# Ten dummy matmuls ahead of the transpose of c and seven behind it, with the ones tile written by VectorE

## Chip, cores and metric

One core of a Trainium2 chip. The metric is the device time of one execution in microseconds (us). Every execution of the experiments is also recorded with its span (first to last instruction, about 1.7 us less than the time) and its mean granted TensorE clock; one execution of each kernel has a full trace.

## The reference

An attention block with sliding-window KV cache and an MLP, both with layer norm modulated by a small vector c. Only the head of it matters here: no projection of x can start before both the normalized x and the modulation from c are there.

```python
mod = (_silu(c) @ w_mod).reshape(c.shape[0], 6, 1, -1)
sa, ca, ga, sb, cb, gb = (mod[:, 0], ..., mod[:, 5])        # cut
h = _layernorm(x, axis=-1) * (1 + ca) + sa
x = x + ga * _A_ref(h, A_k_cache, A_v_cache, A_wq, A_wo)     # 2048 x 512, 32 heads, window 512
h = _layernorm(x, axis=-1) * (1 + cb) + sb
x = x + gb * _B_ref(h, B_w1, B_w2)
```

## The kernel before

Each engine runs its own list, in program order (in the trace before GpSimd has silu at 5.43, 5.80 and 6.92 us, then the pow at 7.08); waits come from the tiles that an operation reads and writes (PE waits 0.73 us for `c_row`). In the views PE is TensorE, PEld its weight loads, DVE VectorE, ACT ScalarE, POOL GpSimd and SP SyncE, which issues loads. This is the opening, up to the first projection (cuts marked). `warm(n)` is n dummy matmuls that keep TensorE busy while the first loads are under way; their result is never read.

```python
def warm(n):
    for i in range(n):
        mm(bank[WBK], ones[:, :], ones[:, 0:1].to_broadcast([P, QB]), True, True, [R_ones], [WBK], i == n - 1)

def silu_exp(bk):                      # c as a row -> c as a column, exp(-c) and c
    cT = bank[bk].bitcast(BF)[:, 0:DC]
    kb.op(PE, ... e.transpose(cT, c_row[:, :], ident[0:DC, 0:DC]) ...)
    kb.op(ACT, ... e.activation(tmp[:, :], cT, ACTF.Exp, scale=-1.0) ...)
    kb.op(ACT, ... e.activation(c_f[:, :], cT, ACTF.Copy) ...)

def silu_mul():                        # three operations on GpSimd
    kb.op(POOL, ... tmp = min(tmp, 1e38) + 1 ...)
    kb.op(POOL, ... tmp = tmp ** -1 ...)
    kb.op(POOL, ... sc_bf = c_f * tmp ...)

# ... loads: x (tiles 0, 1) on SP, x (tiles 2, 3) on ACT, c on SP, then w_mod, wq, k, v
kb.op(POOL, lambda e: e.memset(ones[:, :], 1.0), writes=[R_ones])
# ... identity and other constants on POOL
warm(7)
silu_exp(5)
warm(9)
# ... statistics of x tile 3 on ACT
silu_mul()
ln_stat(0); ln_stat(1); rstd_add(0, 2); rstd_pow(0, 2)   # DVE, DVE, DVE, POOL
ln_stat(2); rstd_add(2, 3); rstd_pow(2, 4)
ln_norm(0); ln_norm(1)                 # DVE: xn of tiles 0 and 1
# ... xn of tile 3 on POOL
ln_tposes(0, TB[0])                    # PE: four transposes of xn, "psS<-ident,xn"
for f in mod_cols_mm(0, QBK): f()      # PE: 32 one-column matmuls, "psQ<-sc_bf,wmw"
# ... modulation, then the first projection, "psQ<-hT,wq", and the first scores
```

GpSimd takes `silu_mul` first and `rstd_pow(0, 2)` after it (at 7.08 us, though the pow's input was there at 6.70), and `ln_norm(0)` waits for that pow. So the first normalized tile waits for c, although it doesn't use it.

Of the kernel before, what the change touches and what calls it, by code (L numbers as in the profile page):

```python
# [1198 lines left out]
def build_fast(nc, es, top, A_x, A_k_cache, A_v_cache, A_wq, A_wo, B_x, B_w1, B_w2, c, w_mod, out, flag):  # L1199
# [28 lines left out]
    def T(name, shape, dt=BF):  # L1228
        return es.enter_context(nc.sbuf_tensor(name, shape, dt))
# [26 lines left out]
    ones = T("ones", [P, P])  # L1256
# [30 lines left out]
    kb = KB(nc)  # L1287
    PE = kb.stream("pe", sem("s_pe"))
    ACT = kb.stream("act", sem("s_act"))
    DVE = kb.stream("dve", sem("s_dve"))  # L1290
    POOL = kb.stream("pool", sem("s_pool"))
# [22 lines left out]
    R_ident, R_ones, R_c, R_sc, R_scf, R_tmp, R_cst = (Res(n) for n in ("ident", "ones", "c", "sc", "scf", "tmp", "cst"))  # L1314
# [27 lines left out]
    def load_v(g, eng=None):  # L1342
        dma(v_sb[:, g, :, 0:Dh], A_v_cache[0][g, Sk - W:, :].rearrange("(k p) d -> p k d", p=P), f"v{g}", writes=[R_v[g]], eng=eng)
# [27 lines left out]
    def mm(out_ap, lhsT, rhs, start, stop, reads, bk, signal):  # L1371
        kb.op(PE, lambda e: e.matmul(out_ap, lhsT, rhs, start=start, stop=stop), reads=reads, group_writes=[R_b[k] for k in bk], signal=signal)  # L1372
# [4 lines left out]
# [3 lines that stand above are left out]
# [34 lines left out]
    def silu_exp(bk):  # L1414
        cT = bank[bk].bitcast(BF)[:, 0:DC]
        kb.op(PE, lambda e: e.transpose(cT, c_row[:, :], ident[0:DC, 0:DC]), reads=[R_c, R_ident], group_writes=[R_b[bk]])  # L1416
        kb.op(ACT, lambda e: e.activation(tmp[:, :], cT, ACTF.Exp, scale=-1.0), reads=[R_b[bk]], writes=[R_tmp])
        kb.op(ACT, lambda e: e.activation(c_f[:, :], cT, ACTF.Copy), reads=[R_b[bk]], writes=[R_cf])
# [146 lines left out]
    load_wq(2, 2)  # L1565
    load_k(0)
    load_v(0)
    kb.op(POOL, lambda e: e.memset(ones[:, :], 1.0), writes=[R_ones])
    kb.op(POOL, lambda e: e.memset(cst[:, 0:1], -0.5), writes=[R_cst])
    kb.op(POOL, lambda e: e.affine_select(ident[:, :], ones[:, :], pattern=[[1, P]], compare_op=ALU.is_equal, fill=0.0,  # L1570
                                          base=0, channel_multiplier=-1), reads=[R_ones], writes=[R_ident])
# [3 lines left out]
    kb.op(POOL, lambda e: e.memset(m01[:, 0:DC], 0.0), writes=[R_m01])  # L1575
    kb.op(POOL, lambda e: e.memset(m01[:, DC:2 * DC], 1.0), writes=[R_m01])
    kb.op(ACT, lambda e: e.activation(cst[:, 2:3], cst[:, 0:1], ACTF.Exp), reads=[R_cst], writes=[Res("dummy")])
    warm(7)
    silu_exp(5)
    warm(9)  # L1580
    t3 = TPB - 1
    kb.op(ACT, lambda e: e.activation(xn[:, t3, :], x_sb[:, t3, :], ACTF.Copy, accum_out=s3[:, 0:1]), reads=[R_x[t3]], writes=[R_xn[t3], R_s3])
    kb.op(ACT, lambda e: e.activation(s3[:, 1:2], s3[:, 0:1], ACTF.Copy, scale=-1.0 / D), reads=[R_s3], writes=[R_s3])
# [217 lines left out]
def bass_adaLN_cond__sliding_block_cached__dense_activation_relu__prompt_kernel(  # L1801
# [14 lines left out]
    with ExitStack() as top:  # L1816
        flag = top.enter_context(nc.sbuf_tensor("flag", [1, 8], mybir.dt.int32))
        with ExitStack() as es:
            kb, fast, cut, dma_cnt, flag_ev = build_fast(nc, es, top, *args, flag)
            sems = dict(kb.sems)  # L1820
            meet = top.enter_context(nc.semaphore("s_meet"))
# [71 lines left out]
```

## Time and profile before

| | before |
|---|---|
| time, the 3 runs known when predicting | 561.12, 560.35, 560.62 us |
| the execution that has the trace | 561.10 us, span 559.4 |
| PE busy | 550.5 us, 98% of the span |
| first dummy / transpose of c / first transpose of xn / first projection | 1.04 / 4.95 / 8.82 / 10.86 us |

In the lines, the first number is the start in us, the second the length; brackets hold idle time of the engine before it and what ended it.

### The profile page before, as it was taken

To read this page: it belongs to the slowest core of one execution; us is meant where nothing else is said; L and a number is where in the kernel's file an instruction comes from. 1 tells how busy PE (TensorE), PEld (TensorE's weight loads), DVE (VectorE), ACT (ScalarE), POOL (GpSimd) and SP (SyncE) were. 2 spreads that over 40 slices of the span, in tenths; PEclk is the share of its full clock that TensorE was granted. 3 is DMA by queue.
4 is the path that set the end of the run, shared out by engine and by line. 5 is a ranking of instruction groups with operands and counts; after the bars stand their busy time and mean duration, and the time that the engine had idled before them with its cause. 6 is when DMAs were issued, how large, how long until landed. Compare 5 with 4: busy or idle time off the path is not lost.

```text
span 559.4 us, 9666 instructions
## 1 busy us (share of the span) xinstructions
PE 550.5 (98%) x4060; PEld 315.8 (56%) x4134; DVE 253.8 (45%) x551; ACT 348.9 (62%) x453; POOL 54.7 (10%) x53
## 2 busy tenths in 40 slices
PE   8999999999999999999999999999999999999998
PEld 4665555555555555555555555555555654444444
DVE  4455555553546544335445443333354448321134
ACT  4986666666666666666666666666666644432500
POOL 3000022004410000033000000332000000000000
DMA  9897763513114144352352412111215110210001
GB/s 268 248 207 174 143 169 46 114 39 76 40 38 76 39 73 117 58 133 57 94 95 57 76 40 39 39 39 38 39 39 76 39 30 0 44 34 23 22 29 47
DMA packets 113309, 42.67 MB, mean 76 GB/s; under 512 B 93928, under 2 KB 112104, under 8 KB 113256
## 3 DMA queue, kind: packets, MB, share of 16 engines
q1 hardware_dynamic: 112024, 40.82, 34.3%
q10 hardware_dynamic: 1232, 1.15, 0.6%
q8 instruction: 33, 0.54, 0.4%
q14 instruction: 20, 0.16, 0.1%
HBM read 18.35 MB, written 2.10 MB: 37 GB/s over the span
## 4 chain that ended last, share of the span: by engine, by line
PE 98%; issue 1%; DMA 1%; DVE 0%; SPq 0%; DVEq 0%
PE psS L1372 28%; PE psO L1372 27%; PE psQ L1372 23%; PE psW L1372 20%; DMA c_row<-in_c_dram 1%; DVE qT L1611 0%; DVE hT L1630 0%; SPq L1303 0%; DVE PT L1723 0%; DVE PT L1725 0%; PE psS L1375 0%; PE psO L1416 0%; DVE modc L1438 0%; DVEq L123 0%
## 5 line engine op out<-in xcount | busy, mean ns | idle before, releaser
L1493 ACT ACTIVATE PT<-psS 128x1024 bf16<-128x1024 f32 x256 | 262.7, 1028 | 128.2 <-PE psS L1372 128.1
L1372 PE MATMUL psS<-qT,kT 128*128 128x512 bf16 x508 | 150.9, 379 | 0.5 <-DVE qT L1611 0.4
L1372 PEld LDWEIGHTS psO<-v,PT 128*128 128x128 bf16 x2048 | 126.6, 98 | 30.2
L1372 PE MATMUL psO<-v,PT 128*128 128x129 bf16 x2048 | 137.0, 220 | 0.0
L1372 PE MATMUL psQ<-hT,wq 128*128 128x512 bf16 (+1 forms) x510 | 130.5, 377 | 0.3 <-DVE hT L1630 0.2
L1503 DVE RECIPROCAL rinv<-psO 128x4 f32<-128x4 f32 x128 | 23.3, 182 | 227.2 <-PE psO L1372 227.2
L1372 PE MATMUL psW<-wo,oT 128*128 128x512 bf16 x454 | 118.1, 379 | 3.0
L1504 DVE TENSOR_TENSOR o<-psO,rinv 128x512 bf16<-128x512 f32 x128 | 88.5, 691 | 4.9 <-DVE rinv L1503 0.5
L1372 PEld LDWEIGHTS psQ<-hT,wq 128*128 128x128 bf16 x512 | 49.9, 98 | 60.3 <-issue 0.6
L1372 PEld LDWEIGHTS psS<-qT,kT 128*128 128x128 bf16 x512 | 49.5, 98 | 58.9 <-ACT PT L1493 0.7
L1485 ACT ACTIVATE qT<-psQ 128x512 bf16<-128x512 f32 x126 | 74.7, 593 | 0.0
L1712 ACT ACTIVATE wq<-psS 128x512 bf16<-128x512 f32 x56 | 33.4, 597 | 49.3 <-PE psS L1372 48.9
L1372 PEld LDWEIGHTS psW<-wo,oT 128*128 128x128 bf16 x512 | 45.0, 98 | 32.9 <-DVE acc L1526 1.2
L1526 DVE TENSOR_TENSOR acc<-psW,acc 128x512 f32<-128x512 f32 x48 | 33.2, 691 | 6.5 <-PE psW L1372 6.5
L1372 PE MATMUL psO<-wmw,wq 128*128 128x512 bf16 (+1 forms) x165 | 32.8, 352 | 0.3
L1529 POOL TENSOR_TENSOR acc<-acc,gaf 128x512 f32<-128x512 f32 x12 | 15.6, 1303 | 146.7 <-DVE acc L1526 139.8
L1388 POOL TENSOR_TENSOR rstd<-rstd,cst 128x4 f32<-128x4 f32 x7 | 7.2, 1025 | 216.8 <-DVE rstd L1387 216.8
L1723 DVE TENSOR_TENSOR PT<-psO,gbf 128x512 f32<-128x512 f32 (+1 forms) x12 | 7.5, 624 | 40.4 <-PE psO L1372 40.4
L1372 PE MATMUL psS<-h2T,wmw 128*128 128x512 bf16 x109 | 25.0, 379 | 0.2
L1372 PEld LDWEIGHTS psO<-wmw,wq 128*128 128x128 bf16 x168 | 15.3, 98 | 16.5
L1372 PE MATMUL psS<-hT,wmw 128*128 128x512 bf16 x110 | 24.4, 379 | 0.1
L1382 DVE BATCH_NORM_STATS2 st<-x 128x6 f32<-128x512 bf16 x31 | 21.1, 681 | 4.8 <-DMA x<-in_A_x_dram 4.8
(85 smaller groups left out, 192.6 us busy)
## 6 DMA issues: line engine op xcount, KB each, us to landing
wo<-in_A_wo_dram SPq DMA_DIRECT2D x4, 1024.0 KB, 5.9
wq<-in_A_wq_dram SPq DMA_DIRECT2D x7, 512.0 KB, 4.6
wmw<-in_B_w_dram SPq DMA_DIRECT2D x14, 256.0 KB, 3.1
wmw<-in_w_mod_dram SPq DMA_DIRECT2D x5, 512.0 KB, 4.8
oT<-o SPq DMA_TRANSPOSE x128, 2.4
out_dram<-PT SPq DMA_DIRECT2D x15, 128.0 KB, 1.7
x<-in_A_x_dram SPq DMA_DIRECT2D x3, 512.0 KB, 4.3
v<-in_A_v_cache_dram SPq DMA_DIRECT2D x8, 128.0 KB, 3.8
```

The lines of the kernel that those rows point to most:

```text
L1372: kb.op(PE, lambda e: e.matmul(out_ap, lhsT, rhs, start=start, stop=stop), reads=reads, group_writes=[R_b[k] for k in bk], signal=signal)
L1382: kb.op(DVE, lambda e: e.bn_stats(st[:, t, :], x_sb[:, t, :]), reads=[R_x[t]], writes=[R_st[t]])
L1388: kb.op(POOL, lambda e: e.tensor_tensor(rstd[:, sl], rstd[:, sl], cst[:, 0:1].to_broadcast([P, hi - lo]), op=ALU.pow), reads=R_rstd[sl] + ...
L1485: kb.op(ACT, lambda e: e.activation(qT[u % NQT][:, :], bank[bk], ACTF.Copy), reads=[R_b[bk]], writes=[R_qT[u % NQT]])
L1493: kb.op(ACT, lambda e: e.activation(PT[u % NPT][:, pr * 2:pr * 2 + 2, :], s_ps[pr][:, :, :], ACTF.Exp, scale=scale), reads=[R_b[pr * 2], R ...
L1503: kb.op(DVE, lambda e: e.reciprocal(rinv[:, u, :], o_ps[:, :, P]), reads=[R_b[5], R_b[6]], writes=[R_rinv])
L1504: kb.op(DVE, lambda e: e.tensor_tensor(o_sb[u % NOS][:, :, :], o_ps[:, :, 0:P], rinv[:, u, :].unsqueeze(2).to_broadcast([P, TPB, P]), op=A ...
L1526: kb.op(DVE, lambda e: e.tensor_tensor(acc[:, tl, :], bank[WBK], acc[:, tl, :], op=ALU.add), reads=[R_b[WBK], R_acc[tl]], writes=[R_acc[tl]])
L1529: kb.op(eng, lambda e: e.tensor_tensor(acc[:, tl, :], acc[:, tl, :], gaf[:, :], op=ALU.mult), reads=[R_acc[tl], R_ga], writes=[R_acc[tl]])
L1712: kb.op(ACT, lambda e: e.activation(h1T[b % 2][:, fc, :], bank[bk], ACTF.Relu), reads=[R_b[bk]], writes=[R_h1[b % 2][fc]], pre=all_events( ...
L1723: kb.op(DVE, lambda e: e.tensor_tensor(yt[i][:, c0:c1], bank[bk][:, c0:c1], gbf[:, c0:c1], op=ALU.mult), reads=[R_b[bk], R_gb], writes=[R_ ...
```

## The change

Its intent, as I read it: no gap in TensorE's dummies while c is on its way, so that the clock opens sooner; that a gap keeps it shut was an estimate, which e1 and e10 test. "Open" is what the traces show as a change of pace: dummies start 0.43 us apart at first ("cold"; 7.59, 8.02, 8.45 in the weight loads of the trace before) and 0.22 us apart later ("hot").

```diff
-    kb.op(POOL, lambda e: e.memset(ones[:, :], 1.0), writes=[R_ones])
+    kb.op(DVE, lambda e: e.memset(ones[:, :], 1.0), writes=[R_ones])
@@
+    warm(10)
+    silu_exp(5)
     warm(7)
-    silu_exp(5)
-    warm(9)
```

## The prediction

> **What bounds the kernel now.** I read the page first: PE is busy for 550.5 of 559.4 us and 98% of the chain that ended last is PE, so the body of the kernel is a stream of matmuls that this change does not touch. Only the opening can move: dummy matmuls and the transpose of c are all issued in the first 9 us. So the second view is the chain of work that ended last, in order of time, for the opening:
>
> ```profile
> 1.24 3.66 DMA c_row<-in_c_dram
> 4.90 0.05 issue
> 4.95 0.18 PE psO L1416
> 5.13 3.86 PE psW L1372 x9
> 8.98 0.22 PE psS L1375 x4
> 9.21 0.79 PE psQ L1372 x32
> 10.00 0.02 issue
> 10.02 0.18 DVE modc L1438
> ...
> 10.30 0.42 DVE hT L1630
> ...
> 10.86 0.78 PE psQ L1372 x4
> ```
>
> Columns: start, length, what. c lands at 4.90 us, PE transposes it, then runs nine dummies (psW), and only then the four transposes of the first normalized tile (psS), the 32 one-column matmuls of the modulation (psQ), their eviction (modc) and the first real projection. So the nine dummies, meant only to warm PE, are on the path for 3.86 us. Was their follower ready earlier? The timeline tells:
>
> ```profile
> 1.04 3.17 PE L1372 MATMUL psW<-ones 128*128 128x512 bf16 x7 [1.04 <-POOL cst L1569]
> 4.95 0.18 PE L1416 MATMUL psO<-ident,c_row 4*128 4x4 bf16 x1 [0.73 <-DMA c_row<-in_c_dram]
> 5.06 3.92 PE L1372 MATMUL psW<-ones 128*128 128x512 bf16 x9
> 5.16 0.17 ACT L1417 ACTIVATE tmp<-psO 128x4 f32<-128x4 bf16 x1 [1.43 <-PE psO L1416]
> 5.43 0.28 POOL L1421 TENSOR_SCALAR tmp<-tmp 128x4 f32<-128x4 f32 x1 [3.17 <-ACT c_f L1418]
> 6.92 0.20 POOL L1423 TENSOR_TENSOR sc_bf<-c_f,tmp 128x4 bf16<-128x4 f32 x1
> 7.08 1.51 POOL L1591 TENSOR_TENSOR rstd<-rstd,cst 128x2 f32<-128x2 f32 x2
> 7.59 0.15 PEld L1372 LDWEIGHTS psW<-ones 128*128 128x128 bf16 x1 [0.28 <-issue]
> 7.82 1.22 DVE L1393 TENSOR_SCALAR xn<-x,mv,rstd 128x512 bf16<-128x512 bf16 x3
> 8.02 0.15 PEld L1372 LDWEIGHTS psW<-ones 128*128 128x128 bf16 x1 [0.28 <-issue]
> 8.45 0.15 PEld L1375 LDWEIGHTS psS<-ident,xn 128*128 128x128 bf16 x1 [0.28 <-DVE xn L1393]
> 8.82 0.39 PE L1375 MATMUL psS<-ident,xn 128*128 128x128 bf16 x4
> 9.04 0.94 PE L1372 MATMUL psQ<-sc_bf,wmw 128*128 128x1 bf16 x32
> ```
>
> The first of three DVE xn takes 0.41 us, so the tile is ready at 7.82 + 0.41 = 8.23, but its transposes start at 8.82: PE is late by 0.59 us, because it is still in dummies. The dummies are slow: weight loads are 0.43 us apart (7.59, 8.02, 8.45). Afterwards PE is about twice as fast: 4 transposes start within 9.04 - 8.82 = 0.22 us, 55 ns each.
>
> [...] By pace the clock opened during the last dummy, near 8.8 us. (The granted clock of the profile says 1.00 everywhere, so it cannot show this.) [...] The trace has no DVE memset to compare; on POOL it is 0.20.
>
> **The change part by part.**
> 1. The ones tile: POOL's 0.20 us at 0.78 goes to DVE, which has nothing to do until x lands at 4.79. Some 0.2 us there too, as small DVE rows take 0.16 to 0.18. The first dummy stays at about 1.04, give or take 0.1. POOL and the identity come no later than now, 3 us before they are needed.
> 2. Ten dummies before c: ten cold ones at 0.427 from 1.04 end at 5.31. c lands at 4.90, so its transpose moves from 4.95 to about 5.31, by +0.36. Gap gone.
> 3. Behind it the c chain moves by that 0.36: exp on ACT, then POOL's silu (5.43 to 7.12), and, since POOL works in order, its pow for rstd at 7.08 (its input, from DVE, was ready at 6.53 + 0.17 = 6.70). So the first xn is ready at 8.23 + 0.36 = 8.59 and its transposes may start at about 8.65.
> 4. Seven dummies behind c: [...] 7 x 0.216 = 1.5 us end near 6.9. Even if all seven stayed cold, 5.4 + 7 x 0.427 = 8.4, still ahead of 8.65. So PE now waits for xn, not xn for PE.
> 5. Sum on the path: transposes at 8.65 in place of 8.82, -0.17 us. Then 0.22 + 0.81 us to modc, as now; DVE's third xn ends at 9.04 + 0.36 = 9.40, before modc at 9.85. POOL's fourth xn (8.70 + 0.90) ends at 9.96, and is used by the last four transposes only, whose consumers sit behind DVE's other hT work. The rest of the opening slides with it: the loads have landed (wq issued at 1.72 took 7.3 us, kT at 2.62 at most 7.2, so 9.0 and 9.8, against uses at 10.8 and 13.1).
> 6. [...] The three times spread over only 0.77 us, so such losses must be rare or small; I allow a further 0.25 us for the median.
>
> Total: 560.62 - 0.17 - 0.25 = 560.2 us.
>
> **Rivals.** (a) The c chain wins: only its delay counts. For it: POOL's silu and pow are serial and begin 0.36 later. Against it: 0.59 us of slack at the transposes. If c lands late or the first dummy starts late, the gain turns into a loss of 0.1 to 0.3: 560.8. (b) PE goes cold again: warm dummies end near 6.9 and PE idles 1.7 us until 8.65[...]: 562. I give this 12%. (c) The whole 0.59 us or more comes out[...]: the transpose of c would then stay near 4.95 and xn near 8.25: 560.0. (d) Nothing is seen, because times of one kernel differ by 0.77 us: likely as to the verdict, and 560.6.
>
> **Range and chances.** The path gains 0.2 to 0.6 us, 0.1% of the time, next to a spread of 0.77. I say 560.2, from 559.4 to 561.0. The whole opening before the first attention scores is 13.3 us, 2.4% of the time; 2% is 11.2 us and cannot be won or lost there by shifting dummies. Hence 0.99 for within 2%, and a half per cent on each side.
>
> **What would show it.** Right: in the timeline of the changed kernel no idle before the transpose of c, which starts at 5.2 to 5.4; dummies behind it 0.22 us apart, from the first or after a few; an idle PE before the first psS transpose, ended by DVE xn, with that transpose at 8.5 to 8.7; POOL's silu beginning 0.3 to 0.4 later than 5.43; the first attention scores (psS from qT, 13.34 now) 0.2 us earlier. Wrong: dummies still 0.43 apart to the end, transposes or half projections at twice their pace (rival b), or first scores at or after 13.34. A move by more than 2 us would have to come from outside the opening, and I would have missed it altogether.

The sum came to 560.62 - 0.17 - 0.25 = 560.2 us. The -0.17 stands on the trace. The -0.25 (executions whose clock opens later, with part of the transposes and projections cold before the change and none after it): read it, like the 562 us of rival (b), as my estimate alone. Rival (c) meant an execution whose ten dummies end before 5.31. The two paces, which differ about twofold for 512 columns, come from the trace before: 0.427 us is a seventh of the time between the weight loads at 5.46 and 8.45, 0.216 a quarter of the 0.86 us of the four 512-column matmuls at 14.59 (`--critical`).

## The result, and the profile after

The changed kernel takes 561.33 us (median of 6 runs, 560.79 to 562.01), the kernel before 560.46 (6 runs, 560.09 to 561.12). The ratio is 1.0014, 95% interval 1.0001 to 1.0027: within 2%, but slower, and outside my range. One of the six has a granted clock of 0.997 (562.01). Ratios here are the mean time of one kernel's fast runs over that of the other's in the same rounds, so not quite the ratio of these medians.

The traced executions say the opposite: 560.80 us after, 561.10 before. The chain of work that ended last, changed kernel:

```profile
1.10 4.24 PE psW L1372 x10
5.34 0.12 PE psO L1416
...
5.48 0.17 ACT tmp L1417
5.66 0.07 ACT c_f L1418
...
5.75 0.28 POOL tmp L1421
...
6.12 1.05 POOL tmp L1422
...
7.24 0.20 POOL sc_bf L1423
7.44 0.67 POOL rstd L1591
...
8.13 0.43 DVE xn L1393
...
8.61 0.40 PE psS L1375 x4
...
10.66 0.78 PE psQ L1372 x4
```

and two rows of its timeline:

```profile
5.38 1.70 PE L1372 MATMUL psW<-ones 128*128 128x512 bf16 x7
8.61 0.40 PE L1375 MATMUL psS<-ident,xn 128*128 128x128 bf16 x4 [1.53 <-DVE xn L1393]
```

Nearly all that I forecast for this trace is there: ten dummies up to the transpose of c, which starts at 5.27 (I said 5.31); the seven behind it at open clock, 1.70 us; PE then idle 1.53 us until xn; its transposes at 8.61 (8.65); the first projection 0.20 us earlier than in the trace before (0.17). And yet the kernel is slower. So I suspected that the trace before is not what the kernel before usually does.

### The profile page after: what moved, and what is told of

Read it like the earlier page. It is cut to its first block, busy times and chain, and to the rows that moved or that the text cites. A ratio compares the mean times of both kernels' runs of the same rounds, so it can differ in the third digit from the quotient of the medians.

```text
span 559.1 us, 9668 instructions
## 1 busy us (share of the span) xinstructions
PE 549.3 (98%) x4061; PEld 315.5 (56%) x4135; DVE 254.1 (45%) x552; ACT 348.9 (62%) x453; POOL 54.6 (10%) x52
## 4 chain that ended last, share of the span: by engine, by line
PE 98%; issue 1%; DVE 0%; POOL 0%; ACT 0%; DVEq 0%; POOLq 0%
PE psS L1372 28%; PE psO L1372 27%; PE psQ L1372 23%; PE psW L1372 20%; POOL tmp L1422 0%; POOL rstd L1591 0%; DVE qT L1611 0%; DVE xn L1393 0%; DVE hT L1630 0%; PE psS L1375 0%; DVE PT L1723 0%; DVE PT L1725 0%; POOL tmp L1421 0%; POOL sc_bf L1423 0%; DVE modc L1438 0%
```

## The experiments

Theories. PIN: usually c is transposed before 4.95 and the dummies behind it run fast, so the chain from c bounds the opening; ten dummies pin the transpose at 5.3. DROP: PE's new idle stretch from 7 to 8.6 us makes the clock fall back in some executions. BODY: the difference lies after the opening. Thirteen experiments ran, three of them repeats of the two kernels, with 5 or 6 timed runs each, all results correct. "Before" stands for runs of the kernel before in the same rounds.

One table of all the traces first, as every experiment is read from it. Times in us; "x" and "c" are the landings of the load of x tiles 0 and 1 and of c, from the trace's record of finished transfers; "cT" is the start of the transpose of c, "xn" of the first ln_norm, "tp" of its first transpose on PE, "proj" of the first projection.

| run | dummies | this execution | x | c | cT | xn | tp | proj |
|---|---|---|---|---|---|---|---|---|
| before | 7/9 | 561.10 | 4.76 | 4.90 | 4.95 | 7.82 | 8.82 | 10.86 |
| after | 10/7 | 560.80 | 5.11 | 4.46 | 5.27 | 8.13 | 8.61 | 10.66 |
| e1 | 7/9 | 560.61 | 4.68 | 4.72 | 4.77 | 7.64 | 8.11 | 10.16 |
| e2 | 10/7 | 561.02 | 4.68 | 4.61 | 5.37 | 8.23 | 8.70 | 10.75 |
| e3 | 10/14 | 561.82 | 4.62 | 4.68 | 5.49 | 8.36 | 9.23 | 11.27 |
| e4 | 7/9 | 560.28 | 4.68 | 4.66 | 4.71 | 7.57 | 8.04 | 10.09 |
| e5 | 7/7 | 560.37 | 4.85 | 4.53 | 4.58 | 7.70 | 8.16 | 10.21 |
| e6 | 10/9 | 560.68 | 4.80 | 4.64 | 5.15 | 8.02 | 8.49 | 10.54 |
| e7 | 13/7 | 562.09 | 4.69 | 4.50 | 6.55 | 9.42 | 9.89 | 11.94 |
| e9 | 8/9 | 560.33 | 4.61 | 4.50 | 4.57 | 7.45 | 7.92 | 9.97 |
| e10 | 4/9 | 561.53 | 4.78 | 4.67 | 4.71 | 7.63 | 8.64 | 10.94 |
| e11 | 7/9, split | 560.47 | 4.77 | 4.48 | 4.53 | 7.62 | 8.08 | 10.13 |
| e12 | 10/7 | 562.09 | 4.76 | 4.93 | 4.97 | 7.84 | 8.31 | 10.36 |
| e13 | 8/7 | 560.43 | 4.76 | 4.63 | 4.68 | 7.61 | 8.07 | 10.12 |

(e8 changes the loads and stands apart below.) In all fourteen rows xn starts 2.84 to 2.87 us after the later of x and cT. Two chains of equal length meet there: x through VectorE's statistics, c through GpSimd. Then tp follows xn by 0.46 to 0.48 us, except in three rows (before, e3, e10), where PE was still in dummies.

### e1 and e2: both kernels again, unchanged

> The kernel before once more, unchanged, for a second trace and the granted clock of every run. Theory PIN (the transpose of c was only as late as in the first trace because c landed late there; in other runs c lands earlier, and the ten dummies of the change pin the transpose at 5.3 us): c lands before 4.9 us here, its transpose starts right after it, first attention scores before 13.34 us, span below 559.4 us, clock 1.000. Theory DROP (in the changed kernel PE idles from 6.9 to 8.6 us and in some runs the clock is taken back): nothing to see in this kernel, clock 1.000 in all runs, median 560.3 to 560.6 us. Theory BODY (the difference lies after the opening): span minus start of first scores differs from 546.0 us.

> The changed kernel once more. PIN: transpose of c at 5.3 us again whatever the landing of c, first scores at 13.1 us again, all runs near 560.8, clock 1.000, so the runs would spread little. DROP: runs split by granted clock; those at 1.000 take 560.8 us, those at 0.997 to 0.999 take 0.5 to 1.3 us more; median about 561.3. BODY: span minus start of first scores above 546.0 us.

e1 took 560.44 us (560.01 to 560.61), e2 560.99 (560.71 to 561.12), all ten runs at clock 1.000; the runs of before alongside 560.50, one of its eleven at 562.07 with clock 0.997. TensorE in the timeline of e1, the same kernel as the trace before:

```profile
1.04 3.17 PE L1372 MATMUL psW<-ones 128*128 128x512 bf16 x7 [1.04 <-POOL cst L1569]
4.77 0.18 PE L1416 MATMUL psO<-ident,c_row 4*128 4x4 bf16 x1 [0.56 <-DMA c_row<-in_c_dram]
4.88 2.13 PE L1372 MATMUL psW<-ones 128*128 128x512 bf16 x9
8.11 0.40 PE L1375 MATMUL psS<-ident,xn 128*128 128x128 bf16 x4 [1.09 <-DVE xn L1393]
```

The nine dummies take 2.13 us, not 3.92: the clock was open when they began, in spite of a gap of 0.56 us. PE is free at 7.0 and waits 1.09 us for xn. So the dummies that I saw on the path aren't there in this execution; the path is c, silu, pow, xn, and it gives the first projection at 10.16, 0.59 before e2's 10.75. That is PIN, to the size: cT is 0.60 later in e2. BODY falls: from the first projection to the end of the last matmul it is 546.05 us in e1 and 545.86 in e2.

### e4: VectorE's memset alone

```diff
-    kb.op(POOL, lambda e: e.memset(ones[:, :], 1.0), writes=[R_ones])
+    kb.op(DVE, lambda e: e.memset(ones[:, :], 1.0), writes=[R_ones])
```

> Only the memset of ones moved to VectorE; 7 and 9 dummies as before. First dummy at 1.10 in place of 1.04 us, seven end 0.06 later, still before c lands, so all theories: same as the kernel before within 0.1 us. If it is slower by 0.5 us or more, the memset is the cause and both PIN and DROP fall.

560.36 us (560.22 to 560.69), ratio to before 0.9997 (0.9984 to 1.0010). The first dummy starts at 1.10 in place of 1.04, the transpose of c at its landing. The interval alone would leave room for 0.56 us; the trace doesn't (first projection at 10.09), and e13 below keeps the memset without the loss. So the memset has no part in it.

### e6 and e7: ten ahead, thirteen ahead

```diff
-    warm(7)          # e6: ones on GpSimd, 9 behind
+    warm(10)
```
```diff
-    warm(10)         # e7: from the changed kernel
+    warm(13)
```

> The kernel before with 10 dummies ahead of the transpose of c in place of 7; 9 behind, memset of ones on GpSimd as before. PIN: c transposed at 5.3 to 5.4, xn and first projection 0.5 to 0.6 later than in the kernel before (10.7 against 10.1), median 561.0, clock 1.000. DROP: PE idles less than in the changed kernel (two dummies more), so nearer to before, 560.5.

> The changed kernel with 13 dummies ahead of the transpose of c in place of 10. PIN: three more dummies at 0.22 (clock open by then) to 0.43 us (not yet open) push the transpose of c to 6.0 to 6.7 us, and every later step of the chain by the same 0.65 to 1.3: median 561.6 to 562.2. DROP: PE idles as long as in the changed kernel; no more slow runs than there, and no other loss, since the last dummy ends before xn is ready: 561.0 to 561.3.

e6: 560.92 us (560.32 to 561.06), before 560.53. e7: 562.35 (562.09 to 562.71), ratio 1.0034 (1.0021 to 1.0047). In e7's chain of work that ended last, everything hangs on the thirteen dummies:

```profile
1.11 5.51 PE psW L1372 x13
...
9.42 0.42 DVE xn L1393
```

The dose fits PIN: cT goes 4.77, 5.15, 6.55 in e1, e6, e7, the first projection 10.16, 10.54, 11.94, so 5.39 after cT each time. e7's median lies a little over the range I gave it: two of its five runs have a dropped clock (0.997; 562.63 and 562.71), and the median of the other three is 562.20, the edge of the range. In its trace the dummies ran cold to the twelfth: cT is 1.28 us later than in the trace after, 0.43 for each of the three dummies more. DROP expected e6 near 560.5 and e7 near 561; both are off.

### e5 and e3: the number behind c

```diff
-    warm(9)          # e5: 7 ahead, ones on GpSimd
+    warm(7)
```
```diff
-    warm(7)          # e3: from the changed kernel, behind c
+    warm(14)
```

> The kernel before with 7 dummies behind the transpose of c in place of 9; all else as before. PIN (what counts is when c is transposed): c transposed when it lands, 4.7 us, first transposes of xn at 8.1, first projection at 10.1; median 560.4, as before. DROP (fewer dummies leave PE idle too long and the clock is taken back): clock below 1.000 in two or more of the runs and 0.5 to 1.3 us more there, median near 561.

> The changed kernel with 14 dummies behind the transpose of c in place of 7: at the open clock they last 14 x 0.217 = 3.0 us and end at 8.4, so PE hardly idles before the transposes of xn at 8.6. DROP: all runs at clock 1.000, none of the slow tail, median 560.8 us (0.5 less than the changed kernel). PIN: no different from the changed kernel in runs of clock 1.000; c still transposed at 5.3. If the clock opens late (after 6.6) in some runs, the dummies reach past 8.6 and cost up to 1 us there.

e5: 560.49 us, before 560.53: fewer behind cost nothing in the median, though one of its six runs has clock 0.997 (561.34) and one 0.999 (560.77). e3: 561.64 (561.20 to 562.56), all at clock 1.000. Filling the idle stretch did not bring back what the change lost, and cost some 0.65 us more than e2: in its trace the clock opened only at 6.8 us (estimated by pace: the 14 dummies start from about 5.60 to 9.02, which is three steps of 0.43 and ten of 0.22), the last of the 14 dummies started at 9.02, and tp is 0.87 after xn, 0.40 more than elsewhere. So the filler had a cost of its own, and e3 alone doesn't settle DROP. e2 does: all its five runs are at clock 1.000, and they lose 0.49 us by the medians all the same.

### e9 and e13: eight ahead

```diff
-    warm(7)          # e9: 9 behind, ones on GpSimd
+    warm(8)
```
```diff
-    warm(10)         # e13: from the changed kernel, 7 behind
+    warm(8)
```

> The kernel before with 8 dummies ahead of the transpose of c. They end at 1.04 + 8 x 0.427 = 4.45 us, still before c lands (4.5 to 4.9 in the seven traces that load it as before). PIN with a threshold: no loss, c transposed at its landing, first projection 5.4 us after it, median 560.3 to 560.5. If dummies ahead cost in any number (0.43 us each, as 10 to 13 would suggest if carried back), 560.7 or more.

> The changed kernel with 8 dummies ahead of c in place of 10, all else as changed (ones on VectorE, 7 behind). PIN: they end at 1.10 + 8 x 0.427 = 4.5, before or just as c lands, so the loss is undone: first projection at 9.9 to 10.2, median 560.3 to 560.5, and 0.5 to 0.7 below the changed kernel of the same rounds. DROP (the seven behind leave PE idle): still about 561.

e9: 560.30 us (560.17 to 560.52), before 560.59. e13: 560.23 (560.12 to 560.43), before 560.56, the changed kernel in the same rounds 561.14 (e12). From e13's timeline:

```profile
1.10 3.51 PE L1372 MATMUL psW<-ones 128*128 128x512 bf16 x8 [1.10 <-DVE ones L1568]
4.68 0.17 PE L1416 MATMUL psO<-ident,c_row 4*128 4x4 bf16 x1
8.07 0.40 PE L1375 MATMUL psS<-ident,xn 128*128 128x128 bf16 x4 [1.59 <-DVE xn L1393]
```

So taking back two of the ten dummies undoes the whole loss, with the memset, the seven behind and the idle stretch (1.59 us) all kept. Eight end at about 4.5 us, when c lands (4.46 to 4.93 in the table); up to there dummies are free, beyond they cost what they last.

### e10: four ahead

```diff
-    warm(7)
+    warm(4)
```

> The kernel before with 4 dummies ahead of c: PE idle from 2.8 us to the landing of c, a longer gap than the 0.7 us of the first trace. Theory LATE CLOCK (the first trace of before was slow because the gap kept the clock shut, so that the nine dummies ran cold on the path): most runs now like the first trace, some or all of the nine dummies 0.43 apart, first transposes of xn later than the xn, first projection 0.4 to 0.7 later than 5.4 us after c, median 560.9 to 561.4. If the dummies ahead do nothing for the clock: 560.4 as before, nine dummies 0.22 apart.

561.01 us (560.53 to 561.53), before 560.59. Its trace shows the slow opening of my first trace again; TensorE in its timeline:

```profile
1.05 1.89 PE L1372 MATMUL psW<-ones 128*128 128x512 bf16 x4 [1.05 <-POOL cst L1569]
4.71 0.18 PE L1416 MATMUL psO<-ident,c_row 4*128 4x4 bf16 x1 [1.78 <-DMA c_row<-in_c_dram]
4.83 4.02 PE L1372 MATMUL psW<-ones 128*128 128x512 bf16 x9
8.64 0.63 PE L1375 MATMUL psS<-ident,xn 128*128 128x128 bf16 x4
```

Here, with a longer gap (1.78 us, against 0.56 in e1 and 0.73 in the first trace), the clock stayed shut, the nine dummies take 4.02 us and PE is late for xn by 0.54 us (8.64 against 7.63 + 0.47). With seven ahead this happens now and then (the first trace), with four in the trace taken here. The other four runs have no trace: 561.47, 561.01 and 560.89 suggest it, 560.53 doesn't.

### e8: c loaded first, and e11: silu split

```diff
+    dma(c_row[:, :], ..., "c", writes=[R_c], eng=ACT)   # e8: ahead of the loads of x
     for i in range(2):
         dma(x_sb[:, 2 * i:2 * i + 2, :], ..., eng=ACT if i else SP)
-    dma(c_row[:, :], ..., "c", writes=[R_c])
```
```diff
     # e11: silu_mul without its last operation, which follows the pow
     rstd_pow(0, 2)
+    kb.op(POOL, ... sc_bf = c_f * tmp ...)
```

> The kernel before with the load of c issued first on ScalarE's queue, ahead of the second half of x. PIN says the chain from c is what the opening waits for: c lands before the seven dummies end, is transposed at 4.1, silu on GpSimd ends at 6.3, and the pow for rstd waits for VectorE's rstd at 6.7 and no longer for silu: xn at 7.4 to 7.5 (7.6 in the repeat of before), first projection 0.1 to 0.2 earlier than 10.1, median 560.2 to 560.3; and with 16 dummies in one stretch no run with a late clock (no 561.1 or above). If the chain from c is not the bound: no change, 560.5, or slower by the 0.4 us that x comes later.

> The kernel before with the last of silu's three GpSimd operations (0.2 us) moved behind the pow for rstd of the first two tiles. PIN names the serial GpSimd chain from c as the bound of the opening: without that 0.2 us in it xn is ready 0.15 to 0.2 earlier, first projection 5.2 after the transpose of c in place of 5.39, median 560.2 to 560.3 (the first modulation matmuls need silu's result only after the first transposes). If GpSimd's order is not on the path: no change, 560.5, 5.39.

Both miss. e8 took 563.00 us (561.42 to 563.45). c is transposed at 4.13 as expected, but the second half of x, now behind c on its queue, lands at 7.7 (4.88 in e1; why an issue 0.60 us later lands 2.85 us later wasn't tested), and VectorE, which works in order, stops at its third statistics ahead of the first ln_norm (that starts at 8.77, though its pow ended at 6.96); two timeline rows:

```profile
7.76 0.69 DVE L1382 BATCH_NORM_STATS2 st<-x 128x6 f32<-128x512 bf16 x1 [1.78 <-DMA x<-in_A_x_dram]
9.23 0.40 PE L1375 MATMUL psS<-ident,xn 128*128 128x128 bf16 x4 [2.87 <-DVE xn L1393]
```

The half of w_mod behind it on the same queue lands at 10.65. So e8 tests the order of loads more than the chain from c. Five of its six runs have a dropped clock (0.996 or 0.997): DROP is real, here with 2.87 us of idle ahead of it (in its trace the seven transposes from 11.12 take 0.91 us, against 0.55 in the changed kernel's first). e11: 560.54, before 560.59: no gain. Its xn starts 2.85 after x. In this execution c landed ahead of x (4.48 against 4.77), so even unsplit the chain from c would have been ready first (4.53 + 2.87 = 7.40 against 7.62): the chain from x, which is as long, was the bound. What the split is worth where c comes last, no trace shows. I had seen only one of the two chains.

### e12: the changed kernel a third time

> The changed kernel a third time, beside the next one. PIN: c transposed at 5.3 to 5.4, xn of the first tile 2.87 later, first projection 5.39 after the transpose; runs at clock 1.000 near 561.0, 0.5 above the kernel before. DROP as a second cause: a run at 0.997 takes about 562.1, and how many of the five show it says whether the first verdict's larger gap (0.87) came from there.

561.14 us (560.98 to 562.09), before 560.56. Four runs at clock 1.000 take 560.98 to 561.40, one at 0.997 takes 562.09, and that one has the trace. Here the clock opened at 3.8 us by the trace's record, the ten dummies ended ahead of c (at 4.75, against 5.34 in the changed kernel's first trace), and cT is not pinned (4.97, at its landing). But the table by stage (columns: stretch, its length, busy time and instructions of PE, weight loads, VectorE, ScalarE, GpSimd, then granted clock, DMA share, GB/s) and two timeline rows show what followed:

```profile
8.00:10.00 2.00, 1.69 (x48) 1.70 (x48) 1.35 (x5) 0.22 (x1) 1.51 (x2) 1.00 1.37 211
10.00:11.00 1.00, 0.82 (x8) 0.40 (x6) 1.00 (x4) 1.00 (x3) 0.00 (x0) 0.81 1.08 338
...
12.00:13.00 1.00, 1.00 (x7) 0.69 (x6) 0.00 (x0) 0.38 (x1) 0.00 (x0) 0.50 1.16 310
...
14.00:15.00 1.00, 0.96 (x4) 0.32 (x4) 0.35 (x2) 0.54 (x1) 0.00 (x0) 0.98 1.10 347
```
```profile
8.31 0.40 PE L1375 MATMUL psS<-ident,xn 128*128 128x128 bf16 x4 [1.53 <-DVE xn L1393]
11.05 1.91 PE L1372 MATMUL psO<-hT,wq 128*128 128x256 bf16 x8
```

By the trace's record of the clock it falls to a half from 10.63 to 14.04 us, over the projections: eight of them take 1.91 us (1.04 in the changed kernel's first trace). From the first projection to the end of the last matmul this execution needs 547.3 us, 1.5 more than e2. So DROP exists. But it isn't the change's doing as far as these runs tell: 0.997 occurs in 2 of 16 runs of the changed kernel and in 4 of 40 runs of the kernel before that ran beside the experiments. (e7, with the same idle stretch, has it in 2 of 5; e13, in none of 5.)

## Why the prediction was wrong

Taking the runs of before beside the experiments and all runs of the changed kernel, and leaving out the six dropped ones (clock 0.997), before has a mean of 560.49 us (36 runs), the changed kernel 561.08 (14), eight dummies ahead (e9 and e13) 560.29 (10). The loss to explain is 0.59 us, give or take 0.17 by the spread of these runs (with the dropped runs in, 0.53). The intervals of single rounds are wider: the ratios of e2 (1.0006, 0.9993 to 1.0019), e6, e10 and e12 include 1, so none of them proves a loss alone. The argument rests on the pooled means and on the traces.

- **The step that failed is the path, "what bounds the kernel now".** "The nine dummies, meant only to warm PE, are on the path for 3.86 us" was true of one slow execution. In e1 the nine take 2.13 us, and in e1 and e4 PE waits 1.1 us for xn. The slack of 0.59 us that I gave to the chain from c is zero there, so its delay counts in full. (Even in the first trace it was 0.53: in most other traces tp follows the start of xn by 0.47, not by the 0.41 that I subtracted.) Of the five traces with seven dummies ahead and the loads as before (before, e1, e4, e5, e11) only the first shows the dummies on the path.
- **Step 6, when the clock opens, is why I took it for the rule**: it had the clock open as late as in the trace before (by pace near 8.8 us), or later, in the other executions too. That was my estimate, shown by no trace. In e1 the clock was open at 4.88, after seven dummies that end at 4.2 and a gap of 0.56 us. I took the spread of 0.77 us as a sign that openings later than the first trace's are rare; the first trace was itself the late case.
- **The sum is the second failure**: the -0.17 belongs to the traced execution, at 561.10 us; I took it from the median, 560.62. From its own base it gives 560.93, and the changed kernel takes 561.08. The further "0.25 us for the median" has the wrong sign.
- **Steps 1 to 5 hold in their sizes, for the traced pair.** Memset 0.17 us, first dummy at 1.10; cT +0.32 against +0.36 in the first pair of traces; POOL's silu 0.32 later; seven hot dummies in 1.70 us (I said 1.5); first projection -0.20 against -0.17.
- **The rival that came true is (a)**, the chain from c, which I priced at 560.8 and tied to a late c or a late first dummy. Neither is needed. The delay is 5.3 less the later of x and c (4.7 in e1 and e4): 0.6 us, which passes whole to xn, projection and end.
- **Rival (b)**, the clock falling back, occurs in both kernels (2 of 16 against 4 of 40 runs), so my 12% met its rate, but not as an effect of the change; its price, 562 us, my estimate, was right: dropped runs are about 1 us above the mean of the others in the changed kernel (562.01 and 562.09) and 1.5 to 2.2 in the one before; (c) is half seen in e12, where the ten dummies end at 4.75 and cT stays at 4.97.
- **Within 2%**, at 0.99, was right for the reason given: 13 us of opening can't hold 11.

Left open: why the first six runs of the changed kernel are higher (561.33) than the ten later ones. One had a dropped clock; two at 561.57 with clocks 0.999 and 1.000 have no trace, and the later rounds ran on four chips. Why the clock opens early in some executions and late in others is open too: the length of the gap is a candidate (0.56 us in e1, 0.73 in the first trace, 1.78 in e10), but not the whole of it, as with dummies and no gap it opened at 3.8 us in e12, and not before the twelfth dummy in e7. The kernel with eight ahead is the best seen, 0.3 us below before in both its rounds, but each interval includes 1 (e13: 0.9991, 0.9977 to 1.0005), so it is not shown to be faster.

## What to carry to other kernels

Before subtracting from a trace, see which of the timed executions it is: here it was the slowest of three, with another bound than the next trace, and a second trace of the unchanged kernel would have told. Filler work in an in-order engine is free only until the next real instruction behind it is ready; count it to that arrival (eight here: 560.23 us in e13, against 561.14 with ten in the same rounds), not past it. And where two chains of nearly equal length meet, delaying one past the other costs in full, while shortening one alone gains at most what it lags the other (0.11 us in e1, where x's would have been ready at 4.68 + 2.85).
